# One more token block by seven half-size products, one mask operation for two key blocks, and loads listed with more reserve

## The chip, the cores and the metric

The kernel runs on one core of a Trainium2 chip. The metric is the device time in microseconds (us) of one execution. TensorE (PE) multiplies matrices into the eight PSUM banks; VectorE (DVE) and ScalarE (ACT) read PSUM and do everything elementwise; GpSimd (POOL) and SyncE (SP) here only issue DMAs.

## The reference

Banded attention over 8 batches of 8 heads, 576 positions, head size 64, then a two-layer network on the 4608 tokens of width 512:

```python
scores = (1/8) * q @ k.T ; masked to |i-j| <= 32 ; attn = softmax(scores)
x = (attn @ v)  laid out as [4608, 512]
h = x @ w_in                 # 512 -> 2048
g = relu(h) ** 2
out = g @ w_out              # 2048 -> 512, float32
```

All inputs are float32; the kernel converts to bf16 on loading and accumulates in float32.

## The kernel before

**Attention.** Each batch is cut into three groups of 192 positions, 24 groups G in all. For a group the K and Q pieces are loaded through POOL's DMA queue into `raw` (`load_qk`, L370), V into `v` (`load_v`, L396). K and Q are turned to head-major `kq`: in the first nine groups by PE (`turn_pe`, L429), later by transposing DMAs that SP issues (`turn_dma`, L455). `scores` (L495) makes the scores of 128 keys by 128 queries for eight heads, for two key blocks A and B of each group. ACT takes the exponential into `e` (L518, 128x1024), DVE multiplies it with the 0/1 band mask into `pt` (L526, 128x1024), one operation per key block. PE multiplies by V (`pv`, L554), DVE normalises (L568, L572), and the result goes transposed into `xt`: by PE in the first nine groups (L594, L600), by SP's transposing DMAs after that (L613, L616).

**First product.** `mm1` (L653) makes h for a block of tokens, 128 of the 2048 features at a time: blocks of 192, 192, 192, 192 and 256 tokens, then blocks of 512. For a 512-token block that is 16 feature blocks by 4 matmuls of 128x512. ACT or DVE takes the relu into `rt` (L629 ACT, L628 DVE); DVE or ACT squares two of them in one operation into `gt` (L624 DVE, L623 ACT). For the blocks named in `MM1S` (tokens 2560, 3072, 3584, 4096) `mm1s` (L733) is used instead: a Winograd form that splits tokens, width and features in two and needs seven half-size products instead of eight. It is 4 slices by 7 products by 4 matmuls of 128x256. Its price is elementwise work: four differences of `xt` (`xs`, L705), a copy of the first product into the second bank (L772/L773), copies of two partial products to `oe` (L634/L633), two additions per slice (L757), a relu of 1024 columns in SBUF (L763 DVE, L764 ACT), and the relus and squares of the other two quarters. The differences of the weights (`sw`, L693) are made once.

**Second product.** The first four 128-token tiles use `mm2` (L798), all later 512-token groups use `strassen` (L880), the same seven-product form with sums of `gt` (L848), and DVE or ACT evacuates (L903, L634, L912); ACT or SP issues the stores.

**What sets the order.** Nothing is scheduled at run time. `rec` records every operation with an engine, an expected duration, and what it reads and writes. A list written into the kernel (`ORDER`) gives for each recorded operation its engine letter (P, A, D, G for POOL, S) and a due time in ns, and then the slot of each buffer taken from a pool. `apply` sorts by due time; `emit` writes each engine's stream in that order and adds semaphore waits only where an operation reads or overwrites another's data. So the due times fix the order on each engine and the buffers, and data fix the rest. `fill` puts idle 128x128 matmuls (L295) where the list leaves PE free in the opening. `slack`, from `LSLACK` and `TSLACK`, is time that the planner behind the list set aside between a load and its reader; it is not in the program. Some buffers are reused as a ring: `NRAW`=4 slots of K and Q, `NV`=5 of V, `NPT`=3 of `pt`, `NRT`=8 of `rt`, `NOE`=6 of `oe`.

`wash` (L858) adds one 128x512 matmul with zeros where the list marks a bank pair with "w".

Of the kernel before, what the change touches and what calls it, by code (L numbers as in the profile page):

```python
# [4 lines left out]
ACTF = mybir.ActivationFunctionType  # L5
# [6 lines left out]
NTOK = B_ * S_  # L12
# [9 lines left out]
    MM1S=(2560, 3072, 3584, 4096),  # L22
# [9 lines left out]
    PAIR=(),  # L32
# [5 lines left out]
    SQP=1,  # L38
    FP=1,
    MP=0,  # L40
# [5 lines left out]
    NPT=3,  # L46
# [4 lines left out]
    LSLACK=300,  # L51
# [177 lines left out]
class Gen:  # L229
# [144 lines left out]
    def load_hw(self, t, g, eng, cast, u0, key):  # L374

        s, h = self.source(t, 0, g)
        for j in range(2):
# [4 lines left out]
            self.p.rec(eng, lambda e, j=j, f=f: e.dma_start(f.rearrange("p (h d) -> p h d", h=8), s[:, j]),  # L382
                       writes=[tag], dma=(f"h{t}{g}{j}", g), key=key, dur=450, move=(h // 2, 16), name=f"h{t}{g}{j}")
            fn = (lambda e, f=f, raw=raw: e.activation(raw, f, ACTF.Copy)) if cast == "ACT" else \
                (lambda e, f=f, raw=raw: e.tensor_copy(raw, f))
            self.p.rec(cast, fn, reads=[tag], writes=[self.rtag(t, 0, g, j)], key=self.cfg.get("CKEY", -100.0 - 14 + 100) + 3 * g,
                       dur=620 if cast == "ACT" else 600, name=f"c{t}{g}{j}")
# [13 lines left out]
    def load_w1(self, d, key):  # L401
        src = self.w_in[:, 512 * d:512 * d + 512].rearrange("(f p) c -> p f c", p=128)
        self.p.rec("POOL", lambda e: e.dma_start(self.W1[:, :, 512 * d:512 * d + 512], src),
                   writes=[("w1", d)], dma=(f"w1{d}", 0), key=key, dur=780, move=(32, 82), name=f"w1{d}")
# [232 lines left out]
    def mm1(self, t0, n, ds, key, pair=False):  # L637
# [7 lines left out]
        v = Virt("bank", nb, clean=c >= 512, where=self.cfg.get("MB"))  # L645
        for h in range(nb):
# [10 lines left out]
            self.p.rec("PE", f, reads=[("xt", s) for s in steps] + [("w1", d // 4) for d in dh[:1]], writes=[(v, h)], uses=[v], key=key + 0.25 * h,  # L657
# [26 lines left out]
    def sums_w1(self, key):  # L684
        w, s, p = self.W1, self.SW, self.p
        for c in range(2):
            lo, hi = slice(512 * c, 512 * c + 512), slice(1024 + 512 * c, 1536 + 512 * c)
            a11, a12, a21, a22 = w[:, 0:2, lo], w[:, 2:4, lo], w[:, 0:2, hi], w[:, 2:4, hi]
            r1, r2 = [("w1", c)], [("w1", 2 + c)]
# [6 lines left out]
    def mm1s(self, t0, key):  # L696
# [11 lines left out]
        for m in range(4):  # L708
# [5 lines left out]
            wl, wh = [("w1", m // 2)], [("w1", 2 + m // 2)]  # L714
# [92 lines left out]
    def store(self, u, oe, dst, src, key, move):  # L807
# [3 lines left out]
                       move=move, name=f"st{u}", alt=("SP", 450, lambda e: e.dma_start(dst, src())), bias=self.cfg["STB"], after=self.stores[n - 8] if n >= 8 else None)  # L811
# [77 lines left out]
    def strassen(self, g, key):  # L889
# [5 lines left out]

        def out(i, j, rd, add, src, k, name):
            u = 4 * g + 2 * i + j
            oe = Virt("oe")
            o = lambda: self.oe(oe)
            if add is None:  # L900
# [139 lines left out]
D900 G1350 A1350 D1800 D8113 D8713 D9423 D10498 D8513 D10898 D12154 D7993 D7873 D9623 D10198 D7488 D7588 D21300 D10608  # L1040
D9908 D7198 D10298 D11118 D12354 D8313 D8933 D9223 D21953 D21015 D22183 D44470 D22063 D29378 S1350 D6598 S900 D4366
G1700 G2488 G4064 G5640 G4852 G3276 G7956 G7216 A900 A5559 A1780 A9625 G6428 G8696 G9580 G10464 G11348 G12128 G14572
G12908 G20264 G16140 G13688 G15352 G21044 G22564 P7268 A7873 P8259 A8811 P9715 A10350 D11468 P10140 A12274 D14614
P12224 D13658 D13928 A14839 P15537 D16007 D16277 P16505 P17033 A17473 P11390 D12554 P10907 A11459 P13176 A13811 D15299
P14929 A16155 D17918 P16245 D16963 D17233 A18287 P19037 D19507 D19777 P19957 P20612 D21400 P13601 A15447 P10565 D13106
P20187 A21580 D22968 P17263 A18896 D22283 P25578 D26810 D27080 D27836 P28708 D29178 D29498 P28478 P30288 D30735 G19428
G17756 G16920 G18592 G27236 G28860 P33757 D34560 P33362 A34221 P40217 A42666 D43784 P18377 D20463 P35676 A37267 D38385
P19297 A21085 D26258 P46188 D46979 D47249 A48111 P48822 D49292 D49562 P49946 P50726 D51819 P20958 D25705 P21618 D28331
D30183 P29628 A30805 P28968 A32115 D32700 P23598 D24468 G24084 G25660 G26448 G24872 G29744 G35150 P44350 D45741 P44982
A45534 P24258 A25245 A35637 P46448 A47083 D48487 P22278 A23148 P48397 A49815 D50933 P22938 D23808 A24430 P50466 D51619  # L1050
D52371 A53483 P54589 D55059 D55944 P59677 P60567 D61324 P27158 A28028 D31973 D39070 D39756 D42365 D40994 D43050 D44570
D46294 P26498 A28612 A33406 P27818 D33322 D35179 D33875 D35935 D36690 D25020 D55259 D31288 D41679 P30518 A35143 A36452
P24918 A25788 G23344 G21824 G30628 G31368 G47604 G49324 P44692 D45255 P50176 A50843 P25838 A26708 A31300 P51820 A52455
D54161 P39557 D40441 P54164 A54799 D56630 P43690 A44996 D47935 P56373 D57315 D57585 D58341 P59417 D59887 D60639 P61457
P61687 D62429 P32042 A32912 P34152 A46348 D53609 P40642 A44501 P36101 P36965 P38693 P47533 A49214 A87336 P46873 A48719
# [121 lines left out]
```

## Time and profile before

| | |
|---|---|
| median of three runs (lowest to highest) | 288.42 us (288.42 to 288.72) |
| the profiled execution's own time | 288.32 us |
| its span, first to last instruction | 286.5 us |
| time outside the span | 1.8 us |
| busy, PE / DVE / ACT / POOL | 281.2 / 228.2 / 200.3 / 117.4 us |
| granted PE clock | 1.000 |

The views used: busy time per engine; groups of instructions by line and form (count, busy time, mean ns of one, idle time before); waits by engine; the chain of work that ended last, in order of time (start us, length us, what); the timeline; busy time in chosen stretches; durations of one line. Matmuls are pipelined, so the mean of one matmul includes its latency; the pace is read from long runs in the chain.

### The profile page before, as it was taken

To read this page: it belongs to the slowest core of one execution; us is meant where nothing else is said; L and a number is where in the kernel's file an instruction comes from. 1 tells how busy PE (TensorE), PEld (TensorE's weight loads), DVE (VectorE), ACT (ScalarE), POOL (GpSimd) and SP (SyncE) were. 2 spreads that over 40 slices of the span, in tenths; PEclk is the share of its full clock that TensorE was granted. 3 is DMA by queue.
4 is the path that set the end of the run, shared out by engine and by line. 5 is a ranking of instruction groups with operands and counts; after the bars stand their busy time and mean duration, and the time that the engine had idled before them with its cause. 6 is when DMAs were issued, how large, how long until landed. Compare 5 with 4: busy or idle time off the path is not lost.

```text
span 286.5 us, 7547 instructions
## 1 busy us (share of the span) xinstructions
PE 281.2 (98%) x3063; PEld 225.6 (79%) x3063; DVE 228.2 (80%) x427; ACT 200.3 (70%) x301; POOL 117.4 (41%) x153
## 2 busy tenths in 40 slices
PE   7999999999999999999999999999999999999995
PEld 7889857788657775667566888888988888888884
DVE  1878978868978798686998989988898978697731
ACT  2875738869783965777787978895688966778420
POOL 8999526999831927694332846000000000000000
PEclk9999999999999999999999999999999999999999
DMA  9999999999999999999999999995201221401033
GB/s 147 158 206 193 188 176 156 155 149 147 177 154 226 134 154 185 159 164 155 134 192 213 174 166 146 173 174 140 55 3 39 55 57 38 149 0 39 11 135 113
DMA packets 171106, 38.60 MB, mean 135 GB/s; under 512 B 158272, under 2 KB 170560, under 8 KB 171072
## 3 DMA queue, kind: packets, MB, share of 16 engines
q0 software_dynamic: 121920, 18.98, 99.4%
q1 hardware_dynamic: 42656, 13.51, 26.3%
q10 hardware_dynamic: 6496, 5.64, 7.2%
q8 instruction: 24, 0.39, 0.6%
q14 instruction: 10, 0.08, 0.2%
HBM read 38.80 MB, written 9.44 MB: 168 GB/s over the span
## 4 chain that ended last, share of the span: by engine, by line
PE 94%; DMA 2%; ACT 2%; DVE 1%; issue 0%; SPq 0%; DVEq 0%; ACTq 0%
PE ps L880 34%; PE ps L653 25%; PE ps L733 17%; PE ps L798 5%; PE ps L495 5%; PE ps L554 4%; DMA ts<-in_k_dram 2%; PE ps L429 2%; PE ps L295 1%; ACT kq L440 1%; PE ps L600 1%; PE ps L594 1%; DVE rt L757 0%; DVE rt L763 0%; ACT e L518 0%; DVE xa L572 0%
## 5 line engine op out<-in xcount | busy, mean ns | idle before, releaser
L653 PE MATMUL ps<-xt,w 128*128 128x192 bf16 (+2 forms) x512 | 77.4, 299 | 0.0
L629 ACT ACTIVATE rt<-ps 128x512 bf16<-128x512 f32 (+1 forms) x93 | 51.6, 566 | 30.1 <-PE ps L653 18.9
L653 PEld LDWEIGHTS ps<-xt,w 128*128 128x128 bf16 x512 | 44.6, 98 | 19.8
L396 POOL DMA_DIRECT2D v<-in_v_dram x48 | 41.9, 882 | 31.2 <-PE ps L554 31.2
L518 ACT ACTIVATE e<-ps 128x1024 bf16<-128x1024 f32 x48 | 48.1, 1021 | 8.3 <-PE ps L495 6.4
L880 PE MATMUL ps<-w,gt 128*128 128x256 bf16 x384 | 47.2, 273 | 0.0
L634 ACT ACTIVATE oe<-ps 128x512 f32<-128x512 f32 x56 | 32.6, 595 | 20.4 <-PE ps L880 10.9
L370 POOL DMA_DIRECT2D raw<-in_k_dram x46 | 36.8, 809 | 22.2 <-DMA kq<-raw 11.4
L623 ACT ACTIVATE gt<-rt 128x1024 bf16<-128x1024 bf16 (+2 forms) x49 | 41.6, 859 | 2.7 <-DVE rt L628 1.7
L880 PEld LDWEIGHTS ps<-w,gt 128*128 128x128 bf16 x384 | 36.7, 98 | 5.5
L526 DVE TENSOR_TENSOR pt<-e,mask 128x1024 bf16<-128x1024 bf16 x48 | 32.5, 685 | 8.5 <-ACT e L518 8.2
L370 POOL DMA_DIRECT2D raw<-in_q_dram x46 | 37.0, 812 | 5.2 <-DMA kq<-raw 2.9
L880 PE MATMUL ps<-ts,ss 128*128 128x256 bf16 x256 | 31.7, 273 | 0.0
L880 PE MATMUL ps<-ts,gt 128*128 128x256 bf16 x256 | 31.6, 273 | 0.0
L880 PEld LDWEIGHTS ps<-ts,ss 128*128 128x128 bf16 x256 | 24.7, 98 | 4.2
L880 PEld LDWEIGHTS ps<-ts,gt 128*128 128x128 bf16 x256 | 24.7, 98 | 3.5
L733 PE MATMUL ps<-xs,sw 128*128 128x256 bf16 x192 | 25.5, 273 | 0.0
L624 DVE TENSOR_TENSOR gt<-rt 128x1024 bf16<-128x1024 bf16 (+2 forms) x43 | 24.4, 576 | 1.3 <-ACT rt L629 1.1
L757 DVE TENSOR_TENSOR rt<-ps,oe 128x512 bf16<-128x512 f32 x32 | 21.6, 684 | 4.2 <-PE ps L733 3.8
L554 PEld LDWEIGHTS ps<-v,pt 128*128 128x128 bf16 x384 | 17.4, 98 | 3.9 <-DVE ps L579 0.8
L733 PEld LDWEIGHTS ps<-xs,sw 128*128 128x128 bf16 x192 | 18.5, 98 | 2.2
L554 PE MATMUL ps<-v,pt 128*128 128x65 bf16 x384 | 19.8, 194 | 0.1
(70 smaller groups left out, 370.2 us busy)
## 6 DMA issues: line engine op xcount, KB each, us to landing
out_dram<-oe ACTq DMA_DIRECT2D x20, 256.0 KB, 4.1
v<-in_v_dram POOLq DMA_DIRECT2D x32, 128.0 KB, 6.7
out_dram<-oe SPq DMA_DIRECT2D x16, 256.0 KB, 3.2
w<-in_moe_w_in_dram POOLq DMA_DIRECT2D x4, 512.0 KB, 9.6
w<-in_moe_w_out_dram POOLq DMA_DIRECT2D x4, 512.0 KB, 16.8
raw<-in_q_dram POOLq DMA_DIRECT2D x18, 96.0 KB, 6.2
raw<-in_q_dram POOLq DMA_DIRECT2D x14, 112.0 KB, 6.1
raw<-in_k_dram POOLq DMA_DIRECT2D x14, 112.0 KB, 6.5
```

The costliest lines, as they stand in the source:

```text
L370: self.p.rec("POOL", lambda e, j=j, dst=dst: e.dma_start(dst, s[:, j]), writes=[self.rtag(t, b, g, j)], dma=(f"{t}{G % self.cfg['NRAW']}{j ...
L396: self.p.rec("POOL", lambda e, j=j, lo=lo, hi=hi, k0=k0: e.dma_start(vt[lo - k0:hi - k0, j, :, 0:64], self.v[b, :, lo:hi, :].rearrange("h ...
L518: last = self.p.rec("ACT", lambda e, ef=ef, v=v: e.activation(ef(), self.bank(v, 0, 2), ACTF.Exp, scale=0.125), reads=[v], writes=tags, ke ...
L526: self.p.rec("DVE", lambda e, pf=pf, ef=ef, mb=mb, n=n: e.tensor_tensor(pf(y=0, n=n), ef(y=0, n=n).rearrange("p (w h q) -> p w h q", w=n, ...
L554: mm = e.matmul(ps[z:z + n, c:c + 65], ptt[:, 4 * (h % 2) + h // 2, z:z + n], vt[:, w, h, 0:65], start=((w == 0 or (z == 64 and split)) an ...
L623: alt = ("ACT", act(c), lambda e: e.activation(dst, src(), ACTF.Square)) if self.cfg["ALT"] else None
L624: self.p.rec("DVE", lambda e: e.tensor_tensor(dst, src(), src(), ALU.mult), reads=rd, writes=wr, key=key, dur=dve(c), name=name, alt=alt, ...
L629: return self.p.rec("ACT", lambda e: e.activation(dst(), src(), ACTF.Relu), reads=rd, writes=wr, key=key, dur=act(c), name=name, alt=alt, ...
L634: self.p.rec("ACT", lambda e: e.activation(dst(), src(), ACTF.Copy), reads=rd, writes=wr, key=key, dur=act(c), name=name, alt=alt, bias=se ...
L653: mm = e.matmul(ht[:, n * x:n * x + n], self.W1[:, ft, 128 * d:128 * d + 128], self.XT[:, ft, r:r + n], start=(ft == 0 and x == 0), stop=( ...
L733: mm = e.matmul(bk[:, 256 * x:256 * x + 256], lhs(k, 256 * m + 128 * x), rhs[:, k, :], start=start and x == 0 and k == 0, stop=(k == 1), s ...
L880: mm = e.matmul(op[:, 256 * y:256 * y + 256], lhs[:, l0[0] + k, a:a + 128], rhs[:, r0 + k, c0:c0 + 256], start=start and y == 0 and k == 0 ...
```

## The change

1. `MM1S` gains token 2048: this block goes from `mm1` to `mm1s`.
2. `PAIR=(1536,)`: in the block of tokens 1536 two feature blocks go into two adjacent banks and one relu of 1024 columns takes both.
3. `MP=1`: from the seventh group on (`NSPLIT`=6), the exponentials of key blocks A and B go into two adjacent slots of `e`, and one DVE operation of 2048 columns applies both masks. `NPT` goes from 3 to 4, so `pt` holds two such pairs.
4. `LSLACK` goes from 300 to 2500, and the whole `ORDER` list is new: other due times, other engines for some evacuations, other slots. 
5. Code without effect at these settings: `W1H` (half loads of w_in) is empty, `TAIL` is 0. `load_hw` can take an engine for each half.

```diff
-    MM1S=(2560, 3072, 3584, 4096),
+    MM1S=(2048, 2560, 3072, 3584, 4096),
-    PAIR=(),
+    PAIR=(1536,),
+    W1H=(),
+    TAIL=0,
-    MP=0,
+    MP=1,
-    NPT=3,
+    NPT=4,
-    LSLACK=300,
+    LSLACK=2500,
...
-            self.p.rec("PE", f, reads=[("xt", s) for s in steps] + [("w1", d // 4) for d in dh[:1]], writes=[(v, h)], uses=[v], key=key + 0.25 * h,
+            got = self.p.rec("PE", f, after=got, reads=[("xt", s) for s in steps] + [("w1", d // 4, d % 4 // 2 if d // 4 in self.cfg["W1H"] else 0) for d in dh[:1]], writes=[(v, h)], uses=[v], key=key + 0.25 * h,
...
 ORDER = """
-D900 G1350 A1350 D1800 D8113 D8713 D9423 D10498 D8513 D10898 D12154 D7993 D7873 D9623 D10198 D7488 D7588 D21300 D10608
...
+D900 G1350 A106595 D2200 D2000 D7498 D10818 D11088 D1800 D9363 D12926 D7718 D10698 D9803 D10598 D7398 D2705 D20999
...
```

What the new list does to the streams, by count of instructions:

| | before | after |
|---|---|---|
| PE 128x512 matmuls of `mm1` | 192 | 128 |
| PE 128x256 matmuls of `mm1s` | 448 | 560 |
| PE zero matmuls of `wash`, 128x512 | 1 | 2 |
| PE idle matmuls 128x128 | 158 | 154 |
| DVE masks of 1024 / of 2048 | 48 / 0 | 12 / 18 |
| DVE additions of `mm1s` (128x512) | 32 | 40 |
| DVE differences `xs` (128x512) | 16 | 20 |
| relu of 1024 in SBUF, DVE / ACT | 10 / 6 | 20 / 0 |
| relu from PSUM on DVE: 512 / 384 / 1024 | 20 / 7 / 0 | 11 / 12 / 1 |
| relu from PSUM on ACT: 512 / 384 / 1024 | 68 / 25 / 0 | 53 / 20 / 7 |
| squares on DVE: 512 / 768 / 1024 | 13 / 9 / 21 | 15 / 9 / 23 |
| squares on ACT: 512 / 768 / 1024 | 19 / 7 / 23 | 25 / 7 / 16 |
| copies to `oe`, DVE / ACT | 12 / 56 | 13 / 63 |
| copies from bank to bank, DVE / ACT | 4 / 20 | 2 / 26 |

POOL issues the same loads, in another order. In the opening one V load goes behind the first quarter of w_in, and all four quarters of w_out go ahead of the second batch's K and Q. The last load of K, Q and V is due at 186.9 us in the list instead of 176.1 us; between 135.9 and 154.0 us the new list has no load due, where the old one has six.

More of the change, by code (lines that the diff above doesn't have):

```diff
@@ L894, in strassen @@
         u2, p5 = Virt("oe"), Virt("oe")
+        last = self.cfg["TAIL"] and g == NTOK // 512 - 1
         def out(i, j, rd, add, src, k, name):
@@ L1045 @@
[L1045 to L1054, printed above, removed]
@@ L1144 @@
+0 1 5 0 4 3 2 0 1 4
 """
```

227 lines of the change are left out of this document (127 added, 100 removed), and 12 rows, old and new, of the table ORDER.

## The prediction

> **What bounds the kernel now.** I read the busy times first, then who waits on PE, then the chain that ended last in order of time.
>
> ```profile
> span 286.5 us, 7547 instructions
> PE 281.2 (98%) x3063; PEld 225.6 (79%) x3063; DVE 228.2 (80%) x427; ACT 200.3 (70%) x301; POOL 117.4 (41%) x153
> PEclk9999999999999999999999999999999999999999
> PE 94%; DMA 2%; ACT 2%; DVE 1%; issue 0%; SPq 0%; DVEq 0%; ACTq 0%
> ```
>
> PE is busy for 98% of the span and 94% of the last chain, at full granted clock. A busy PE need not be at its pace, so I look at long runs in the chain (start, length, what) and at the waits of PE and of its weight loads.
>
> ```profile
> 137.48 3.45 PE ps L653 x16
> 171.07 3.51 PE ps L733 x32
> 226.85 2.62 PE ps L733 x24
> 263.97 19.23 PE ps L880 x176
> 283.28 0.60 ACT oe L634
> ```
>
> ```profile
> PE ps L295 <- DVE zz L289: 1.2, 1, 1.2
> PE ps L429 <- DVE raw L385: 0.5, 1, 0.5
> ```
>
> ```profile
> PEld ps L798 <- DMA w<-in_moe_w_out_dram: 0.5, 1, 0.5
> ```
>
> The two PE waits fall into the first 7 us; one more shows on the weight loads, for a quarter of w_out. Sixteen matmuls of 512 columns take 3.45 us, 0.216 each; twenty-four of 256 columns take 2.62, 0.109 each; the last 176 matmuls run at 19.23 / 176 = 0.109 without a hole, up to 283.2 us. So from some 18 us on the end is set by the number of matmul columns, and by nothing else but small holes. The largest late hole is in the chain between 174 and 179 us:
>
> ```profile
> 174.68 0.69 DVE rt L757
> 175.40 0.71 DVE xa L572
> 176.12 1.06 DVE rt L763 x2
> 177.22 0.70 DVE rt L757
> 177.97 0.61 PE ps L733 x4
> ```
>
> Here PE waits for a bank that DVE empties: four matmuls of 0.109 are 0.44, the piece is 0.61 long with the latency of the last one, and the chain runs through DVE before it. From the starts of the neighbouring matmuls I put the hole at 0.25 us. It is the one place where DVE sets the end, and it matters below.
>
> **The change part by part.** The sum goes against the profiled execution's own 288.32 us, 0.10 below the median of the three runs.
>
> *Tokens 2048 by seven products.* 64 matmuls of 512 columns go, 64 x 0.216 = 13.82; 112 of 256 columns come, 112 x 0.1092 = 12.23. PE: **-1.59**. All of it is on the path, since PE has no hole to put it in.
>
> ```profile
> L858 PE MATMUL ps<-zz 128*128 128x512 bf16 x1 | 0.4, 379 | 0.0
> L295 PE MATMUL ps<-zz 128*128 128x128 bf16 x158 | 12.2, 235 | 1.2 <-DVE zz L289 1.2
> ```
>
> A second washing matmul comes: same form as the 0.216 ones, **+0.22**. Four idle matmuls fewer stand in waiting time of the opening: 0.
>
> The elementwise work of that block grows. The rows that I need, for DVE and then for ACT:
>
> ```profile
> L526 DVE TENSOR_TENSOR pt<-e,mask 128x1024 bf16<-128x1024 bf16 x48 | 32.5, 685 | 8.5 <-ACT e L518 8.2
> L757 DVE TENSOR_TENSOR rt<-ps,oe 128x512 bf16<-128x512 f32 x32 | 21.6, 684 | 4.2 <-PE ps L733 3.8 <-ACT oe L634 0.2
> L628 DVE TENSOR_SCALAR rt<-ps 128x512 bf16<-128x512 f32 x20 | 13.5, 684 | 1.9 <-ACT rt L629 0.9 <-PE ps L653 0.8
> L848 DVE TENSOR_TENSOR gt<-gt,ss 128x2048 bf16<-128x2048 bf16 x8 | 9.7, 1218 | 0.8 <-PE ps L880 0.8
> L624 DVE TENSOR_TENSOR gt<-rt 128x1024 bf16<-128x1024 bf16 x21 | 14.4, 685 | 0.8 <-ACT rt L629 0.6
> L624 DVE TENSOR_TENSOR gt<-rt 128x512 bf16<-128x512 bf16 x13 | 5.4, 419 | 0.5 <-ACT rt L629 0.5
> L763 DVE TENSOR_SCALAR rt<-rt 128x1024 bf16<-128x1024 bf16 x10 | 4.3, 451 | 0.1
> L705 DVE TENSOR_TENSOR xs<-xt 128x512 bf16<-128x512 bf16 x8 | 3.3, 419 | 0.0
> ```
>
> ```profile
> L518 ACT ACTIVATE e<-ps 128x1024 bf16<-128x1024 f32 x48 | 48.1, 1021 | 8.3 <-PE ps L495 6.4 <-DVE kq L441 0.9 <-ACT oe L634 0.5
> L629 ACT ACTIVATE rt<-ps 128x512 bf16<-128x512 f32 x68 | 39.8, 595 | 17.7 <-PE ps L653 9.3 <-PE ps L733 6.6 <-DVE gt L624 1.1
> L623 ACT ACTIVATE gt<-rt 128x1024 bf16<-128x1024 bf16 x23 | 24.2, 1055 | 1.7 <-DVE rt L628 0.8 <-DVE rt L763 0.7
> ```
>
> A block by `mm1`: 16 relus x 0.595 + 8 squares x 0.685 = 15.0. By `mm1s`: 8 relus x 0.595, 12 copies x 0.595, 8 squares of 512 x 0.419, 4 of 1024 x 0.685, 8 additions x 0.684, 4 relus in SBUF x 0.451, 4 differences x 0.419 = 27.0. So 12.0 us more for DVE and ACT together. Cost on the path: 0 while both have room; if that cover goes, see the second rival.
>
> *Masks in one operation.* 36 masks of 0.685 become 18 of 2048 columns. No such mask was run; the product of the same size in the sums of `gt` took 1.218. The bounds are 0.685 (nothing for the second half) and 2048 columns at the pace of the PSUM relu, 0.684 x 4 = 2.74. I take 1.218, because it has the same width, types and place, and because the present mask costs what a plain 1024 product costs (0.685 both), so its repeated mask is free already. DVE: 18 x (1.370 - 1.218) = -2.7 us. The multiply by V of key block A now waits for the exponential of B and for a mask longer by 0.53, that is 1.02 + 0.53 = 1.6 us later. Behind it in PE's stream stand other matmuls that the new list puts there, and the fourth `pt` slot lets the next pair be made meanwhile: 0 on the path, up to 0.3 in each of a few groups if not.
>
> *One relu for two banks at tokens 1536.* 16 relus x 0.595 become 8, which I price as the exponential of the same shape, 1.021: -1.35 on ACT, 0 on the path.
>
> *All engines.* By the counts in the table of the change, DVE gains 8 additions (+5.5), 10 relus in SBUF (+4.5), 4 differences (+1.7), squares (+2.9), loses 9 relus of 512 (-6.2) against 5 of 384 and one of 1024 (+4.0), the masks (-2.7) and small copies (-1.4): about +8, to 236 of 285 us. ACT loses about 5, to 195. PE stays the bound.
>
> *Loads with more reserve.* Who waited for loads of the later batches?
>
> ```profile
> POOL v L396 <- PE ps L554: 31.2, 5, 10.4
> POOL raw L370 <- DMA kq<-raw: 14.3, 3, 10.8
> ```
>
> POOL waits for buffers; PE never for these loads. So more reserve gains nothing that is now lost; it protects. The opening is another matter: the queue carries the same loads in a new order, w_out ahead of the second batch.
>
> ```profile
> L403 POOL DMA_DIRECT2D w<-in_moe_w_in_dram x4: 800/805/839, 10.9 to 14.0; - x4
> DMA to landing us min/median/max: 6.7/9.6/13.0
> ```
>
> Four quarters of w_in are issued within 3.1 us and land 6.7 to 13.0 us later, so the queue is full and a load's landing follows from the bytes ahead of it. Ahead of the last quarter of w_in these are the same; one V load less stands ahead of the first. I take 0, with 0.5 either way, the size of the one wait for w_out above.
>
> *The relus in SBUF beside loads.* Of the ten L763 operations one was slow:
>
> ```profile
> L763 DVE TENSOR_SCALAR rt<-rt x10: 406/418/736, 176.1 to 262.9; 128x1024 bf16<-128x1024 bf16 x10
> ```
>
> ```profile
> 174.94 1.67 POOL L396 DMA_DIRECT2D v<-in_v_dram  x2
> ```
>
> The slow one is the first, at 176.12, and POOL was making up its last loads until 174.94 + 1.67 = 176.61. The other nine came after POOL had ended and took 0.42. The 0.32 us lost stand directly ahead of PE's 0.25 hole. The Trainium skill ("SBUF — State Buffer", section "SBUF: two separate sides") says that a DVE operation on both of its ports and a POOL operation exclude each other for a whole instruction, and that POOL can't write DMA descriptors meanwhile; by that rule, which speaks against this change, relus in SBUF should be kept away from loads, and the trace agrees with it in this one case (0.736 against 0.418). In the new list 20 such relus stand on DVE, and by due times four of them beside a load, since tokens 2048 come earlier and the loads end later. If each passes 0.25 us on to PE, that is 1.0; if none, 0. I take half of them, **+0.5**, and the old hole's **-0.25** goes.
>
> Sum: -1.59 + 0.22 - 0.25 + 0.50 = -1.12, so 288.32 - 1.12 = **287.2 us**. After PE's last matmul come the same copy and store as before.
>
> **The rivals.**
>
> 1. *DVE and POOL collide more often.* For: the row above; DVE has little to catch up with where tokens 2048 and 2560 follow each other. Against: one case only. If all eight relus of these two blocks lose 0.32 and all of it reaches PE, 2.6 in place of 0.5: 289.3; half of that is likelier, 1.3: 288.0.
>
> 2. *Slower: DVE and ACT run out of room at tokens 2048.* One mechanism, one place: the stage in which that block is made, now 136.4 to 162.5 us, against the stage of tokens 2560, 167 to 190 us (length, PE, PEld, DVE, ACT, POOL).
>
> ```profile
> 136.40:162.50 26.10, 26.10 (x248) 16.91 (x247) 23.64 (x44) 20.73 (x30) 11.43 (x15) 1.00 1.49 171
> 167.00:190.00 23.00, 22.91 (x249) 20.17 (x247) 21.00 (x39) 19.93 (x34) 8.10 (x10) 1.00 2.06 169
> ```
>
> DVE and ACT together do 44.4 us in 52.2. With 12.0 more, less 0.6 for four pairs of masks, it is 55.8: 3.6 too much, 1.8 on each engine if shared evenly, 3.6 if one carries it. It decides from the point where over 7.8 us of the added work stay in the stage. Time: 288.32 - 1.37 + 1.8 to 3.6 = 288.8 to 290.6. Against: the stage at 167 us holds such a block together with scores and second products, DVE and ACT busy 40.9 of 46, and PE lost 0.1; and the list can push work to both sides.
>
> 3. *The opening eats it.* If a w_in or w_out quarter, or the K of the second batch behind all of w_out, lands late by two such waits: +1.0, 288.2.
>
> 4. *The double mask isn't at the pace of the sums.* At 2.74 each, 18 x 1.5 = 27 us on DVE, 263 of 285: DVE would bound long stretches, some 295 us. Nothing in the rows speaks for it.
>
> **How the numbers follow.** Forecast 287.2 with 0.60, its own spread 286.7 (no collision, opening 0.2 better) to 287.8; first rival at some 288.0 with 0.15; second with 0.14; third with 0.08; fourth with 0.03. A measurement can tell some 0.2% from no change: faster means under 287.84, slower over 289.0. Faster: nearly all of the forecast and a third of the first and third rivals, 0.66. Slower: most of the second, the fourth, 0.15. Same: 0.19. The range 286.7 to 288.8 leaves out most of the second rival, the fourth, and a little below.
>
> **What would show it.** Right: PE's last matmul near 282.1 us; L733 in 560 matmuls at 0.109; holes of PE after 18 us no more than some 0.8 in sum; masks of 2048 near 1.22; most relus in SBUF at 0.42 and those beside loads at 0.7. Wrong: PE pieces of the 2048 block stretched with DVE or ACT named ahead of them (second rival); PE waiting on a DMA before 45 us (third); the hole count growing wherever POOL is busy (first).

## The result, and the profile after

The changed kernel takes **290.25 us** (median of 7, 289.2 to 293.99) where the kernel before took 288.70 on the same chip (median of 7, 288.42 to 288.79): ratio 1.005, 95% interval 1.0028 to 1.0071. It is 0.5% slower; forecast was 0.4% faster. (Here and below a ratio leaves out executions over 1.5% above their kernel's fastest, while a median takes all, so a ratio can differ from that of its two medians.) The profiled execution took 290.22 us. Its page:

```profile
span 288.4 us, 7644 instructions
PE 280.8 (97%) x3108; PEld 231.6 (80%) x3108; DVE 237.9 (82%) x431; ACT 197.2 (68%) x295; POOL 117.7 (41%) x153
PEclk9999999999999999999999999999999999999999
PE 86%; DVE 8%; DMA 2%; ACT 2%; issue 1%; DVEq 0%
```

Engine sums came out as forecast (DVE 237.9 for 236, ACT 197.2 for 195), the clock is full, and yet PE's share of the last chain fell from 94% to 86%. So somewhere PE stands and waits. The chain in order of time (start us, length us, what) shows two places. The first, at the third feature block of tokens 1536:

```profile
108.30 0.70 DVE ss L861
109.00 0.20 issue
109.20 2.75 PE ps L666 x12
```

The second, at tokens 3072:

```profile
189.46 5.78 DMA xt<-xb
...
195.53 1.09 DVE xs L718 x3
```

The second place names the releaser plainly: a transpose of `xt`, issued by SP at 189.46, lands at 195.25, and the differences `xs` and then PE wait for it. The first place names DVE, which is a trap: the sums `ss` at 108.30 belong to another block, and nothing that PE is about to do reads them. What these matmuls read is `xt`, and its last transpose shows in the rows of L628 (durations and starts of the issues, then issue to landing):

```profile
L628 SPq DMA_TRANSPOSE xt<-xb x2: 1265/1490/1715, 99.1 to 100.4; - x2
DMA to landing us min/median/max: 8.2/8.4/8.6
```

Issued at 100.4, landed 8.6 us later, at 109.0; PE starts at 109.20. In two further executions (e0 and e4 below) PE also went on 0.25 us behind this landing: 108.16 after 107.91, and 109.05 after 108.81. In before, the last transpose of that block was issued later, at 102.7, and landed earlier, at 108.27 (rows of L616, the shorter of the two flights):

```profile
L616 SPq DMA_TRANSPOSE xt<-xb x2: 1217/1457/1697, 94.8 to 102.7; - x2
DMA to landing us min/median/max: 5.5/6.0/6.4
```

To see what each place costs I took the start of every PE operation less its due time in the list. The lists end at 282.50 us (before) and 281.19 us (after) for PE's last group, so the changed list is 1.31 us shorter. How far PE lags the list ("drift"), and where that changes:

| us | before | after |
|---|---|---|
| drift at 57 us (all of the opening) | -0.37 | +0.39 |
| gained 57 to 104 | -0.08 | +0.23 |
| 104 to 113, tokens 1536 | +0.04 | **+1.47** |
| 113 to 168, tokens 2048 and the start of 2560 | -0.03 | -0.07 |
| 168 to 190 (the old hole at 175) | +0.33 | -0.02 |
| 190 to 200, tokens 3072 | -0.11 | **+1.12** |
| 200 to the end | -0.13 | -0.30 |
| drift at the end | -0.35 | +2.82 |

The drift is 3.17 us worse, the list 1.31 shorter: 1.86 later, and the spans say 288.4 - 286.5 = 1.9. The shorter PE work is there; three stretches take it and more: opening 0.76, tokens 1536 1.43, tokens 3072 1.23.

Why do the transposes of tokens 1536 land late? SP's queue in that stretch (start us, length us, what; a length in which several are joined holds SP's waits):

```profile
85.80 9.00 SPq L467 DMA_TRANSPOSE kq<-raw  x3
94.85 1.25 SPq L625 DMA_TRANSPOSE xt<-xa  x1
96.19 1.52 SPq L467 DMA_TRANSPOSE kq<-raw  x1
97.76 1.25 SPq L625 DMA_TRANSPOSE xt<-xa  x1
99.07 3.02 SPq L628 DMA_TRANSPOSE xt<-xb  x2
```

Three K and Q transposes hold SP from 85.80 to 94.80, since the last of them waits for the K load of batch 4, piece 01, which lands at 93.56 by its own record. The `xt` transposes, whose first norm was done at 92.87, stand behind it. And the transfers are slow there too. From 84 to 109 us, of after: busy tenths of the DMA engines, then packets and MB of POOL's queue (its last figure, a time share, I don't read):

```profile
DMA  9999999999999999959999999999999999999999
q0 software_dynamic: 13559, 1.70, 112.8%
```

and of before:

```profile
DMA  8999999099999875999999999999999939999999
q0 software_dynamic: 10491, 1.32, 96.6%
```

In this stretch the new order of loads puts 29% more packets on POOL's queue, and the pauses of before are gone. How one kind of load, V, landed in the same stretch, after (L399) and then before (L396):

```profile
L399 POOL DMA_DIRECT2D v<-in_v_dram x5: 777/794/915, 87.0 to 108.6; - x5
DMA to landing us min/median/max: 5.8/9.9/11.4
```

```profile
L396 POOL DMA_DIRECT2D v<-in_v_dram x4: 777/831/902, 92.8 to 109.0; - x4
DMA to landing us min/median/max: 3.4/5.3/7.0
```

Two readings fit, then. **Order:** SP works in order, one K or Q transpose waits for a late load, and the urgent `xt` transposes stand behind it. **Bunching:** too many transfers in flight at once, so that each takes 8 us in place of 5.5, whoever is first. The rival to both is the forecast's: DVE or ACT short of time at tokens 2048.

### The profile page after: what moved, and what is told of

It reads as the page before. It is cut to its first block, busy times and chain, and to the rows that moved or that the text cites. A ratio compares the mean times of both kernels' runs of the same rounds, so it can differ in the third digit from the quotient of the medians.

```text
span 288.4 us, 7644 instructions
## 1 busy us (share of the span) xinstructions
PE 280.8 (97%) x3108; PEld 231.6 (80%) x3108; DVE 237.9 (82%) x431; ACT 197.2 (68%) x295; POOL 117.7 (41%) x153
## 4 chain that ended last, share of the span: by engine, by line
PE 86%; DVE 8%; DMA 2%; ACT 2%; issue 1%; DVEq 0%
PE ps L893 30%; PE ps L746 21%; PE ps L666 18%; PE ps L811 5%; PE ps L566 4%; PE ps L507 4%; PE ps L297 3%; DMA xt<-xb 2%; DVE pt L538 2%; PE ps L441 1%; ACT e L530 1%; DVE xa L584 1%; DVE ss L861 1%; PE ps L612 1%; PE ps L606 1%
## 5 line engine op out<-in xcount | busy, mean ns | idle before, releaser
L641 ACT ACTIVATE rt<-ps 128x512 bf16<-128x512 f32 (+2 forms) x80 | 47.6, 606 | 30.0 <-PE ps L666 19.5
L666 PE MATMUL ps<-xt,w 128*128 128x192 bf16 (+2 forms) x448 | 62.0, 288 | 1.4 <-DVE ss L861 1.4
L646 ACT ACTIVATE oe<-ps 128x512 f32<-128x512 f32 x63 | 36.4, 596 | 26.2 <-PE ps L893 16.2
L666 PEld LDWEIGHTS ps<-xt,w 128*128 128x128 bf16 x448 | 38.7, 98 | 15.1 <-ACT e L530 1.6
L399 POOL DMA_DIRECT2D v<-in_v_dram x48 | 42.2, 885 | 16.5 <-PE ps L566 15.9
L635 ACT ACTIVATE gt<-rt 128x512 bf16<-128x512 bf16 (+2 forms) x48 | 37.3, 800 | 3.5 <-DVE rt L640 1.6
L746 PE MATMUL ps<-xs,sw 128*128 128x256 bf16 x240 | 32.9, 273 | 0.0
L538 DVE TENSOR_TENSOR pt<-e,mask 128x2048 bf16<-128x2048 bf16 (+1 forms) x30 | 30.1, 1007 | 1.9 <-ACT e L530 1.4
L770 DVE TENSOR_TENSOR rt<-ps,oe 128x512 bf16<-128x512 f32 x40 | 27.5, 687 | 3.7 <-PE ps L746 2.6
L746 PEld LDWEIGHTS ps<-xs,sw 128*128 128x128 bf16 x240 | 22.8, 98 | 3.0 <-ACT rt L641 0.2
L746 PE MATMUL ps<-xt,w 128*128 128x256 bf16 x160 | 22.5, 273 | 0.7 <-ACT e L530 0.7
```

Source lines behind the costliest of these rows:

```text
L399: self.p.rec("POOL", lambda e, j=j, lo=lo, hi=hi, k0=k0: e.dma_start(vt[lo - k0:hi - k0, j, :, 0:64], self.v[b, :, lo:hi, :].rearrange("h ...
L538: self.p.rec("DVE", lambda e, pf=pf, ef=ef, mb=mb, n=n: e.tensor_tensor(pf(y=0, n=n), ef(y=0, n=n).rearrange("p (w h q) -> p w h q", w=n, ...
L635: alt = ("ACT", act(c), lambda e: e.activation(dst, src(), ACTF.Square)) if self.cfg["ALT"] else None
L641: return self.p.rec("ACT", lambda e: e.activation(dst(), src(), ACTF.Relu), reads=rd, writes=wr, key=key, dur=act(c), name=name, alt=alt, ...
L646: self.p.rec("ACT", lambda e: e.activation(dst(), src(), ACTF.Copy), reads=rd, writes=wr, key=key, dur=act(c), name=name, alt=alt, bias=se ...
L666: mm = e.matmul(ht[:, n * x:n * x + n], self.W1[:, ft, 128 * d:128 * d + 128], self.XT[:, ft, r:r + n], start=(ft == 0 and x == 0), stop=( ...
```

## The experiments

Each kernel was compared with the kernel before on the same chip. Beside the times stands the drift of the profiled execution by stretch, worked out as above (not read for f2 and h1).

| kernel | median us, this / before | ratio, 95% interval | at 57 us | 1536 | 2560 (156 to 168) | 3072 | end |
|---|---|---|---|---|---|---|---|
| after, again (e0) | 290.26 / 288.76 | 1.0049, 1.0028 to 1.0069 | +0.03 | +0.78 | -0.01 | +1.23 | +1.90 |
| after, third time (i0) | 290.49 / 288.41 | 1.0031, 1.0002 to 1.006 | +0.38 | 0.00 | +1.53 | +0.83 | +2.58 |
| e4 | 289.82 / 288.76 | 1.0037, 1.0015 to 1.0058 | -0.16 | +1.87 | -0.01 | -0.07 | +1.49 |
| g1 (before, shorter) | 287.48 / 288.47 | 0.9968, 0.9956 to 0.998 | -0.35 | 0.00 | -0.22 | -0.11 | -1.27 |
| f1 | 287.33 / 288.47 | 0.9962, 0.9943 to 0.9981 | -0.21 | -0.01 | -0.01 | -0.08 | -0.45 |
| g2 (before, less V) | 288.18 / 288.47 | 0.9984, 0.9973 to 0.9995 | -0.14 | 0.00 | 0.00 | -0.11 | -0.43 |
| e1 | 293.84 / 288.76 | 1.0163, 1.0127 to 1.02 | +0.37 | -0.01 | +1.67 | +0.11 | +4.26 |
| e2 | 295.82 / 288.76 | 1.023, 1.02 to 1.0259 | +0.07 | -0.01 | +6.74 | -0.07 | +7.99 |
| f2 | 288.75 / 288.47 | 1.0013, 0.9988 to 1.0039 | | | | | |
| h3 | 289.24 / 288.6 | 1.0008, 0.9975 to 1.0041 | +0.04 | 0.00 | -0.01 | +1.45 | +1.32 |
| h1 | 289.91 / 288.6 | 0.9994, 0.9959 to 1.0029 | | | | | |
| h2 | 289.15 / 288.6 | 1.0007, 0.9981 to 1.0033 | +0.59 | +1.81 | +0.17 | -0.07 | +2.36 |
| e3 | 290.06 / 288.60 | 1.0035, 1.001 to 1.006 | +0.75 | +2.41 | -0.01 | +0.67 | +3.68 |
| i1 | 291.35 / 288.41 | 1.0083, 1.0057 to 1.011 | +0.49 | +1.58 | -0.01 | -0.08 | +1.84 |
| i2 | 289.00 / 288.41 | 1.0006, 0.9988 to 1.0024 | +0.38 | +2.16 | -0.01 | -0.08 | +2.31 |
| i3 | 287.91 / 288.41 | 0.9976, 0.9963 to 0.9988 | +0.21 | 0.00 | -0.01 | -0.07 | -0.02 |
| **j1** | **287.40** / 288.53 | **0.9966, 0.9953 to 0.9978** | -0.37 | +0.52 | -0.01 | -0.07 | -0.08 |
| j2 (before, less idle) | 288.71 / 288.53 | 1.0008, 0.9999 to 1.0017 | -0.37 | 0.00 | 0.00 | -0.10 | -0.37 |

A first thing is in the table's top: the changed kernel is not late at the same place each time. Its three profiled executions lose 1.47, 0.78 and 0 at tokens 1536; 0, 0 and 1.53 at tokens 2560; 1.12, 1.23 and 0.83 at tokens 3072. And it scatters, 287.46 to 293.89 in 12 runs of i0, where the kernel before stayed within 288.07 to 289.64 in 33 (on two other chips single executions of it reached 292.46 and 295.04).

**The changed kernel again (e0, i0), as controls.** No edit.

> The changed kernel once more, unaltered, so that its edits below stand beside it on one chip. In its first trace PE lost, against the order list, 1.4 us at the first product of tokens 1536 (a transposing DMA of xt landed at 108.96 us, PE went on at 109.20) and 1.1 us at tokens 3072 (another landed at 195.25, the differences xs began at 195.53), and began its first transposes 0.8 us later than in the kernel before. Theory T (PE waits for transposing DMAs that stand late in SP's queue): holes again at these two places, of 0 to 2 us each, 288.8 to 291. Theory D (DVE's added work sets the end): holes wherever tokens 2048 and 2560 are made.

> The changed kernel unaltered, on the chip of the three others: 290.0 to 290.5, 0.4 to 0.6% above the kernel before, with a hole on PE ahead of the 9th multiply of tokens 1536 (0.7 to 2.6 us) and one at tokens 3072 (0.5 to 1.2 us).

Measured 1.0049 and 1.0031. In i0 the hole expected at tokens 1536 was not there (its last transpose landed at 107.39); one at tokens 2560 was: PE stood still for 1.25 us, until 164.78. The rows of the transposes of L625 between 150 and 165 us:

```profile
L625 SPq DMA_TRANSPOSE xt<-xa x2: 1301/1438/1574, 149.1 to 157.1; - x2
DVE xs L718: 1.3, 1
DMA to landing us min/median/max: 2.8/4.2/5.7
```

The one issued at 157.1 lands 5.7 later, at 162.8; `xs` waited 1.3 us for it, and PE for `xs`. In the first profiled execution of after the same transpose landed at 162.79 and the `xs` that reads it started at 162.81, so nearly at the same times; but PE was 1.4 us later there, and the stretch lost nothing. So the mechanism is one, a transpose of `xt` that lands after PE is ready for it; what PE doesn't lose at tokens 1536 it can lose at tokens 2560. In i0 a slow relu in SBUF (0.752 us at 163.15, beside a V load that POOL was making up from 162.83) stands between the differences that PE waits for, so some 0.3 us of that hole fit the first rival's mechanism.

The packets on POOL's queue, as counted above, are not the measure of bunching. From 84 to 109 us e0 had more of them than the first execution, and its last two transposes of tokens 1536 were faster:

```profile
q0 software_dynamic: 13873, 1.74, 115.8%
DMA to landing us min/median/max: 5.8/6.2/6.6
```

In i1 below, 11348 packets went with 7.3 to 8.2 us. The number of POOL's loads that are under way during the last transpose's flight, from its issue to its landing (loads issued before it landed that landed after it was issued), goes with the flight's length better: 7 loads in before (5.54 us), 8 in f1 (6.34), 14 in after (8.58), 16 in i1 (8.24), but also 14 in e0 (6.60). SP's own transposes under way at its issue were 1 in before, and 4 in after as in f1; with 4 in both, f1's flight is 2.2 us shorter. These are single executions.

**Is it elementwise work at tokens 2048 (e4)?** The eight additions and the four relus in SBUF of that block are cut to 64 columns, so most of their work is left out (some 4.6 us of DVE).

```diff
+        few = slice(0, 64) if t0 == 2048 else slice(None)
...
-  e.tensor_tensor(hs(), src(), self.oe(u), ALU.add)
+  e.tensor_tensor(hs()[:, few], src()[:, few], self.oe(u)[:, few], ALU.add)
...
-  e.tensor_scalar(src2(), src2(), 0.0, None, ALU.max)
+  e.tensor_scalar(src2()[:, few], src2()[:, few], 0.0, None, ALU.max)
```

> The changed kernel with the eight additions and the four relus in SBUF of the block of tokens 2048 cut to 64 columns: most of that work is left out, some 4.6 us of DVE. Theory D: 1 to 2 us less than the unaltered kernel. Theory T: within 0.3 us of it, with the same two holes.

1.0037: still slower than before. The 1.87 us lost at tokens 1536 lie ahead of this block and can't answer the question; the stretch in which the block is made does: from 113 to 168 us PE lost nothing in after (-0.07), so there was nothing for less DVE work to cure. The rows of after for the two stages that the second rival named agree (length, PE, PEld, DVE, ACT, POOL):

```profile
136.40:162.50 26.10, 26.10 (x294) 22.79 (x293) 23.11 (x39) 21.30 (x35) 6.48 (x8) 1.00 1.46 158
167.00:190.00 23.00, 23.00 (x262) 20.28 (x260) 21.01 (x37) 19.79 (x33) 12.27 (x16) 1.00 1.88 148
```

PE is busy for all of both. DVE has 23.11 us and ACT 21.30 in a stage of 26.10, less on both together (44.41) than I had feared (55.8).

**Does less PE work shorten the kernel at all (g1)?** The kernel before, in which seven of the 64 matmuls of tokens 2048 are left out: 7 x 0.216 = 1.5 us of PE, and no elementwise work, DMA or due time touched.

```diff
-                    for ft in range(4):
+                    for ft in range(3 if t0 == 2048 and d >= 9 else 4):
```

> The kernel before with 7 of the 64 matmuls of 512 columns of the block of tokens 2048 left out: 7 x 0.216 = 1.5 us of PE, nearly the 1.59 that the change takes out of that block, with no elementwise work added and no order changed. If the step of the prediction holds that matmul columns alone set the end: 1.5 us less, 287.2. If the loop of loads and transposes is nearly as long as PE's work in the kernel before too: less than 1 us.

287.48, that is 0.9968, and the span is 1.0 us shorter than in the profile of before:

```profile
span 285.5 us, 7514 instructions
```

The path of the matmuls does set the end, and some 1.0 of the 1.5 us came through.

**Is it the transfers (f1, g2)?** 30 V loads of batches 3 to 7 are cut to 16 rows in the changed kernel (f1) and in the kernel before (g2): the rest of V isn't loaded, all waits stay.

```diff
             lo, hi = max(k0, 0), min(k0 + 128, S_)
+            hi = lo + 16 if b >= 3 else hi
```

> The changed kernel with the 30 V loads of batches 3 to 7 cut to 16 of their 96 or 128 rows (the rest of V is left out), which takes some 20 us of transfer time out of the one queue that POOL fills; order and waits are as they were. Theory T (transposing DMAs and loads form a loop without reserve, PE waits for xt at its end): the holes at tokens 1536 and 3072 close, 287.2 to 288.0, below the kernel before. Theory D (DVE's added work): 290, as without the cut.

> The kernel before with the same 30 V loads cut to 16 rows, as a control. PE shows no wait for a DMA after 45 us there, so by both theories within 0.3 us of the kernel before.

The changed kernel went from 1.0049 to 0.9962, and the holes at tokens 1536, 2560 and 3072 are gone. The kernel before gained 0.16%. In f1 the last `xt` transposes of tokens 1536 took 6.3 to 6.9 us where after's took 8.2 to 8.6:

```profile
L629 SPq DMA_TRANSPOSE xt<-xb x2: 1257/1624/1990, 97.9 to 99.2; - x2
DMA to landing us min/median/max: 6.3/6.6/6.9
```

So the change has its gain, 288.47 - 287.33 = 1.1 us, as soon as the transfers get out of its way; against g2, which also loads less of V, it is 288.18 - 287.33 = 0.85. The failed part of the prediction is in the transfers. f1 doesn't tell order from bunching, since it also makes the late K load earlier (92.34, in after 93.56).

**SP's order (e1, e2, f2).** On SP the `xt` transposes go ahead of the K and Q transposes at tokens 1536 (e2), at tokens 3072 (f2), at both (e1). Due times in the list:

```diff
-S93954 S96494 S97744 S98994 S95204
+S92300 S92600 S95150 S96100 S96200
...
-S182624 S186364 S178162 S180742
+S181900 S185650 S186400 S186500
```

> The changed kernel with nine due times altered on SP alone: the four transposes of xt of groups 9 and 10 stand ahead of two transposes of K and Q that are needed later, and those of group 18 ahead of two others. Nothing is computed otherwise. Theory T: both holes close, 1.4 + 1.1 us less than the unaltered kernel, 287.4 to 288.2. Theory D: no change, within 0.3 us of the unaltered kernel.

> Only the first of the two reorderings on SP, for groups 9 and 10. Theory T: the hole at tokens 1536 closes and the one at tokens 3072 stays, about 1.4 us less than the unaltered kernel. Theory D: no change.

> The changed kernel with only the second reordering on SP: the transposes of xt of group 18 ahead of two transposes of K and Q of batch 7. Theory T: the hole at tokens 3072 (1.0 to 1.2 us) closes, the one at tokens 1536 stays: 288.9 to 289.3. If the loop merely passes the delay on, as the first reordering did, no gain or a loss.

At the place that is treated the hole closes each time: 1536 in e1 and e2 (-0.01), 3072 in e1 (+0.11). (At tokens 3072 that alone proves little: e2, e4 and i1, untreated there, show no hole either, with PE 1.8 us or more behind its list by then. i3 and j1 below, with PE on time, show it: their last transpose landed at 192.10 and 191.68 and nothing was lost, in h3, untreated, at 193.74 and 1.45 was.) But e1 (1.0163) and e2 (1.023) are far slower. POOL waits longer for the `raw` slots that the put-off K and Q transpose releases, and its next loads slide. POOL's timeline of e1 (at the end of a line the wait ahead of it), and of after:

```profile
109.71 1.53 POOL L372 DMA_DIRECT2D raw<-in_k_dram  x2 [5.12 <-DMA kq<-raw]
...
113.46 4.29 POOL L399 DMA_DIRECT2D v<-in_v_dram  x5
```

```profile
108.64 4.31 POOL L399 DMA_DIRECT2D v<-in_v_dram  x5
```

Five V loads come 4.8 us later, and e1 loses 1.70 us between 113 and 140, where its chain runs through one of these loads. e2 loses 1.37 there and then 6.74 at tokens 2560, 4.6 of it ahead of the first product: SP waited until 149.6 for a K load, and the `xt` transpose behind it was issued at 160.65. The other 2.1 are the price of the hole itself: PE stood still for 4.46 us, and from 166.7 to 173.6 the granted clock was 0.50 (below, the third figure from the end):

```profile
169.09:173.56 4.47, 4.46 (x28) 3.29 (x29) 3.24 (x5) 2.18 (x4) 4.22 (x6) 0.50 2.40 154
```

f2 alone is 1.0013, not told apart from before, while e0 was 1.0049. The theory of order fits tokens 3072 and, at tokens 1536, closes the hole but fails as a cure: the delay is handed on.

**POOL's order at tokens 1536 (h3), with SP's at 3072 (h1), with fewer idle matmuls (h2, e3).** Three loads that are due while the `xt` transposes of tokens 1536 are in flight go behind them (first diff: h1, h2 and h3); in h2, and in e3 alone, 56 instead of 71 idle matmuls at the start (second diff).

```diff
-G99656 G101924 G102712
+G106700 G106750 G106800
...
-gap, one = 56 * (39 + max(0, gap - 3900) // 56), 56
+gap, one = 56 * (24 + max(0, gap - 3900) // 56), 56
```

> The changed kernel with only the three loads moved. Theory T: the hole at tokens 1536 (0.7 to 1.8 us) closes, the one at tokens 3072 stays: about 1 us less than the changed kernel, 289.0.

> The changed kernel with the reordering on SP for group 18 and, against the hole at tokens 1536, three loads of batch 5 that are not needed before 133 us (k521, v421, q511) moved on POOL from among those issued at 97 to 101 us to behind ten others; all work stays. Theory T: fewer transfers run when the four transposes of xt of groups 9 and 10 are issued, these land about 2 us earlier, both holes close: 287.4 to 288.2, below the kernel before. If the delay is passed on again: 289 or more, with a new hole.

> The same with 56 instead of 71 idle matmuls at the start. In the traces the slow start of PE's clock takes 27 to 55 of them, 5.5 to 7.0 us for all 71, and the first transposes stand behind them. With 56 they end by 7.2 us at the latest: up to 0.8 us less where the clock comes late, 0 where it comes early; 0.3 to 0.5 less in the median.

> The changed kernel with only 56 instead of 71 idle matmuls at the start. If the 0.8 us by which PE's first transposes began late in its first trace reach the end: 0.3 to 0.5 less in the median. If the later waits for xt take them up: no change.

h3 speaks for bunching: its last `xt` transpose was issued later than in after (101.09 against 100.38) and landed sooner (106.85 against 108.96), with 11 loads under way in place of 14. That is weak evidence, since e0's, unaltered, took 6.60 us from issue to landing where h3's took 5.76. The hole at 1536 is gone in that profile, the one at 3072, not treated, is +1.45. In the median of all runs it is worth less than in the profile: 1.0008. h1 (0.9994) and h2 (1.0007) aren't told apart from before. In h2 the hole at 1536 is back (+1.81), so h3's cure isn't a safe one. e3 alone is 1.0035, not told apart from e0; its earlier start was spent by waiting, first for a quarter of w_in that landed at 21.55 (due 20.68), then at 1536 (+2.41).

**One load ahead of a blocked one (i1).** POOL idles 3.93 us ahead of a V load, for a buffer that PE still reads; the K load of piece 01, whose own buffer is free, stands behind it. It goes ahead.

```diff
-G84555
+G80900
```

> The changed kernel with one load placed earlier on POOL: K of batch 4, piece 01, ahead of a V load for whose buffer POOL idles about 4 us; its own buffer has been free since 73 us. Theory (SP's in-order queue is held by a K transpose that waits for a late load, and the transposes of xt behind it come late): the load lands at 84 to 86 us in place of 92 to 96, SP is no longer held, the last xt transpose of tokens 1536 is issued at about 98 and lands at about 106, the hole at tokens 1536 closes, the one at 3072 stays; 288.7 to 289.3, so 1.0 to 1.5 below the changed kernel beside it. Rival (all transfers together are too many in that stretch, whoever is first): the xt transposes still land at 108 or later and the time is within 0.4 of the changed kernel. Second rival (the hole moves on to the next block that has a just-in-time transpose): the hole at 1536 closes and one as large opens at tokens 2048 or 2560; time within 0.4.

The load landed at 85.58 in place of 93.56, eight us earlier. And the last `xt` transpose of tokens 1536 was issued at 100.92, landed at 109.16, and the hole was +1.58. SP's timeline shows why, and POOL's beside it:

```profile
86.26 8.74 SPq L467 DMA_TRANSPOSE kq<-raw  x3
95.05 1.24 SPq L625 DMA_TRANSPOSE xt<-xa  x1
96.68 1.57 SPq L467 DMA_TRANSPOSE kq<-raw  x1
```

```profile
97.75 1.64 POOL L372 DMA_DIRECT2D raw<-in_q_dram  x2 [10.54 <-DMA kq<-raw]
```

POOL now stops for 10.54 us for a slot of `raw` (6.68 in after), so all that it gained it gives back. The third transpose was issued earlier, but SP stays with K and Q until 95.00, and the next such transpose now waits for the next load, Q of piece 20, which landed at 96.62 (11.0 us after its issue, 9.1 in after). The transfers took longer, and the end stayed. My theory in its form "one late load holds SP" fell with this run: 1.0083, no better than the changed kernel beside it (1.0031). But i1 didn't issue the last `xt` transpose any earlier, so it doesn't test whether that would help; e2 and j1 do.

**The cure in three places (i2), with 56 idle matmuls (i3).** i1's edit; SP's order at tokens 3072 as in f2; and ahead of tokens 2560 the K and Q loads of piece 01 of batch 6, and two more, go ahead of a load for whose slot POOL idles.

```diff
-G128475 G129263 G132559 G134279
+G113400 G113500 G119000 G119100
```

> The same earlier load, and the same cure at the two other places where the xt transposes are late or just in time: at tokens 3072 the two xt transposes ahead of two K and Q transposes on SP; ahead of tokens 2560 the load and transpose of K of batch 6, piece 01, ahead of a Q load for whose buffer POOL idles. Theory: no hole is left at 1536, 2560 and 3072, and what is left of the sum is the shorter PE work against the later opening: 287.3 to 288.0, 0.2 to 0.4% below the kernel before. Rival (general load of the transfers): 289.5 or more, with holes at other blocks.

> The three places and 56 in place of 71 idle matmuls at the opening. If the holes are gone, a start 1.0 us earlier is kept to the end in part: 286.9 to 287.8. If transposes of xt are again what PE waits for, the earlier start is used up by the next hole: as the run without it, within 0.3.

At tokens 2560 the cure holds: the K load lands at 132.73 in place of 144.79, its transpose is issued at 140.88 and not at 144.81. In i3 the last `xt` transpose of that block lands at 157.56, 3.0 us ahead of the `xs` that reads it, where after had 0.02; in i2, late from tokens 1536 on, the margin is 0.4. At 3072 no hole is left in i2 or i3 (nor in i1, which has no edit there). At 1536 i2 still lost 2.16, which is its whole lag. i3 lost nothing there in its profile, and it is **faster than before**: 0.9976. Why fewer idle matmuls help here and not in e3 the profiles don't show: the hole at 1536 comes and goes from run to run.

**Four places (j1), and a control (j2).** One more step at tokens 1536: the one `xt` transpose whose norm is done goes ahead of the K and Q transpose for which SP waits anyway; the three that follow it keep their order. j2 is the kernel before with 56 idle matmuls.

```diff
-S96494
+S95190
```

> The three places, 56 idle matmuls, and one xt transpose of tokens 1536 put ahead of the K and Q transpose for which SP waits (its norm was done 1.9 us before SP waits; the K and Q transpose goes behind it and its readers come 20 us later). Theory of the two causes at tokens 1536 (SP waits in order for a late load, and the transfers there are bunched): the last xt transpose is issued 1.0 to 1.3 earlier and lands by about 105.5 to 108 in place of 106.6 to 109.6, the hole left there in some executions closes: 287.2 to 287.7, 0.3 to 0.4% below the kernel before, and less scatter than the three places alone. Rival (only the bunching counts, an earlier issue just takes longer): as the three places with 56 idle matmuls, 287.7 to 288.2.

> The kernel before with 56 in place of 71 idle matmuls at the opening, nothing else: a control for the versions that have this edit. If the opening decides nothing later in the kernel before, it gains up to 0.3 (its idle stretch lasted 5.5 us in the profile shown, not 7.0); if its just-in-time transposes of xt take the gain up, it is within 0.2% of before. If it gains as much as the three places with 56 idle matmuls do, 0.2% or more, then those owe their gain to the opening and not to the change.

j1: 287.40, **0.9966**, and its five runs lie within 287.11 to 288.10. j2: 1.0008, so fewer idle matmuls alone give the kernel before nothing; j1 and i3 owe their lead to the change with its transfers in order. The span on j1's page, and SP between 94 and 101 us:

```profile
span 285.5 us, 7614 instructions
```

```profile
93.87 2.56 SPq L625 DMA_TRANSPOSE xt<-xa  x2
96.53 1.25 SPq L467 DMA_TRANSPOSE kq<-raw  x1
97.82 2.78 SPq L628 DMA_TRANSPOSE xt<-xb  x2
```

Two `xt` transposes now go out together at 93.87, and the K and Q transpose is no later than in i1. The last one, issued 1.1 earlier than after's, took 7.99 us, so it landed 1.7 earlier; j1's chain still runs through it:

```profile
99.26 7.99 DMA xt<-xb
...
107.48 2.75 PE ps L666 x12
```

As many loads were under way during its flight as in after, 14. So bunching is still there, and the hole is 0.52, at a PE that is 0.75 us earlier by then than after's. j1's interval overlaps i3's: that j1's extra step adds to i3 is not shown.

## Why the prediction was wrong

**PE work: right.** -1.59 + 0.22 were forecast, -1.37; the list got 1.31 shorter, g1 shows that a shorter PE stream reaches the end (1.0 of 1.5 us), and j1 ends 1.0 us of span ahead of before.

**The old hole at 175 us: right.** Forecast -0.25, drift there from +0.33 to -0.02.

**Masks: right.** Forecast 1.218 us each and nothing on the path; the row of L538 (shortest, median, longest):

```profile
L538 DVE TENSOR_TENSOR pt<-e,mask x30: 681/1214/1226, 11.7 to 228.8; 128x2048 bf16<-128x2048 bf16 x18, 128x1024 bf16<-128x1024 bf16 x12
```

**Relus in SBUF beside loads: wrong by size.** I took +0.50. The row:

```profile
L776 DVE TENSOR_SCALAR rt<-rt x20: 415/420/577, 150.5 to 266.7; 128x1024 bf16<-128x1024 bf16 x20
```

The slowest of the 20 lost 0.16, not 0.32 on several, and PE had no hole there. The first rival, which needed 1.3 us of PE's time, falls with it. The rule that the prediction cites from the Trainium skill ("SBUF — State Buffer", section "SBUF: two separate sides") is not refuted, since single slow ones occur: 0.752 us in i0, where it lengthened a hole by some 0.3, and 0.864 in i3, where PE lost nothing. Not every one beside a load is slow: the one at 163.15 in after took 0.45. It counts for little here.

**The second rival: fell** (the rows of both stages, and e4). The fourth fell with the masks.

**The opening: mis-sized.** I took 0 with 0.5 either way; it cost 0.76 in the profiled execution and 0.40 and 0.75 in the two others, all of it scattered: in eleven other versions of the changed kernel in the table the drift at 57 us lies between -0.37 and +0.75. Part of it is the idle matmuls ahead of the first turn. Before, and after:

```profile
1.20 5.45 DMA ts<-in_k_dram
7.19 0.58 PE ps L429 x8
```

```profile
1.19 6.97 PE L297 MATMUL ps<-zz 128*128 128x128 bf16 x71 [1.19 <-DVE zz L291]
```

Before, a load ends the wait ahead of the first turn, at 7.19; after, the same number of idle matmuls lasted until 8.16, and the chain runs through them. PE goes through them at half its later pace at first, and the change of pace came later in after. From 4 to 6 us, before and then after (the first count in brackets is of matmuls):

```profile
4.00:6.00 2.00, 2.00 (x38) 2.00 (x36) 0.43 (x1) 0.63 (x1) 2.00 (x3) 1.00 1.48 191
4.00:6.00 2.00, 2.00 (x22) 2.00 (x20) 0.43 (x1) 0.63 (x1) 2.00 (x3) 1.00 1.46 206
```

With 56, j1's first turn began at 7.18, but j2 shows that the number alone gives nothing where the load comes last.

**The failed step** is "PE never [waits] for these loads. So more reserve gains nothing that is now lost; it protects", costed at 0. I looked for who waits on a load, and found only POOL. The loads are read by SP's transposes, in order, and behind them, in the same queue, stand the transposes of `xt`, which PE reads with margins of tenths of a us (in the kernel before: landed 108.27, read 108.41). I priced the moved loads by who reads them and not by what they share a queue and the DMA engines with, and priced the moved transposes on SP not at all. In the new list the last `xt` transpose of tokens 1536 goes out earlier than before (100.4 against 102.7), but behind three more of SP's transposes and beside twice as many loads, and takes 8.58 us in place of 5.54: it landed at 108.96 where PE was ready at 107.77. The price was 0.8 to 1.5 at tokens 1536 or 2560 and 0.8 to 1.2 at tokens 3072, more in sum than the gain of 1.3. No rival of mine had it. That the transposes set PE's end is shown (the chain at 3072, the landings at 1536 and 2560), and f1 against g2 shows that the transfers are the cause. Why a transpose takes longer is only argued: fewer loads under way went with shorter flights in f1 and h3, but three executions of the same kernel took 8.58, 6.60 and 7.77 us.

**What stays open.** How the loss divides between a late issue and a long flight was not settled: against the first execution of after, e2 and j1 got their landing earlier mostly by the one, h3 by the other, f1 by both. How much of the bunching comes from `LSLACK` and how much from the rest of the new list was not separated, since the list is one. Some 0.3 us of drift between 57 and 104 us are in nearly every version of the changed list (in after one step, at 59.5 us), and I did not follow them. A version that puts h3's loads off as well as j1's four edits was not run.

## What to carry to other kernels

A transfer that moves earlier is not free because its reader has time: ask what shares its queue and its DMA engines, and how much margin the just-in-time transfers behind it have, to the tenth of a us. When curing one wait shows the next, look at the sum of lags over the whole run rather than at single holes: e1, e2 and h3 each closed the hole that they aimed at and ended no faster than the kernel before. In an in-order queue, put the urgent transfer ahead of the one with 20 us to spare, and see in the trace which buffers that puts off.

## What the runs showed of the hardware

- A transposing DMA of `xt` on SP took from 2.3 to 8.6 us from issue to landing within one profile of after, by its place in the stream; the same one (the last of tokens 1536) took 8.58, 6.60 and 7.77 us in three executions of the same kernel.
- The packets on POOL's queue from 84 to 109 us don't tell how long it takes: 10491 of them with 5.5 us (before), 11348 with 8.2 (i1), 13559 with 8.6 (after), 13873 with 6.6 (e0).
- Issuing one transposing DMA kept SP for 1.2 us in the median of the 60 in after, and for up to 3.3, so that four of them in a row are 5 us of SP or more.
- The chain of waits named DVE for a wait that a DMA ended (at 109.00, the landing at 108.96). Where the named engine's operation has nothing to do with the waiting one, look up what the waiting one reads.
- The 71 idle matmuls at the start took 5.51 us in the profile of before and 6.97 in that of after: PE did 22 matmuls from 2 to 4 us in both, and from 4 to 6 us 38 in before and 22 in after. The pages give a full granted clock for these slices all the same.
- A long hole can cost more than its length: in e2 PE stood still for 4.46 us, the granted clock was 0.50 from 166.7 to 173.6 us, and 2.1 us more were lost. A hole of 2.57 us in e3 left it at 1.00.
